# Moving three small second-layer matmul groups behind the last first-layer product of a step

## The chip, the cores and the metric

The kernel runs on one core of a Trainium2 chip. TensorE (PE) multiplies, with its weight loads (PEld) as a stream of their own; VectorE (DVE) and ScalarE (ACT) do everything elementwise; SyncE (SP) issues the DMAs. The metric is the device time of one execution in microseconds, as the median of several runs; less is better.

## The reference

```
qn = q / (norm(q, axis=1) + 1e-6);  kn = k / (norm(k, axis=1) + 1e-6)   # q, k, v: (4, 6080, 256)
s = kn^T @ qn / tau;  a = softmax(s)                                     # 256 x 256 for each batch
x = (v @ a).reshape(24320, 256)
h = x @ w_in                                                             # 256 -> 2048
g = 0.5 * h * (1 + erf(h / sqrt(2)))
out = g @ w_out                                                          # 2048 -> 256
```

For each of four batches a channel attention gives a 256 x 256 matrix; the attended values then pass a feed-forward layer with an exact GELU. All of it is in float32.

## The kernel before

The attention matrix is multiplied into `w_in` once for each batch, so that per token only two products are left: a first layer, `v` by the folded weights (256 to 2048), and a second layer, the GELU's output by `w_out` (2048 to 256). Every float32 operand is split into a high and a low part of a narrower format, and each product is three matmuls: high by high, high by low, low by high.

The tokens of a batch are cut into six pairs of column blocks, of 512 columns each (480 in the last pair). A pair is worked in eight **steps**, each for 256 of the 2048 hidden units. In all but 17 of the 192 steps the first layer uses a Strassen-Winograd scheme: seven products instead of eight 2 x 2 block products. The seven products are numbered 0 to 6 here; `first_products` issues them, three matmuls each, into two PSUM banks in turn (tile `h` in the profile). Products 0, 2, 4 and 6 accumulate in the bank `one`, products 1, 3 and 5 in the bank `two`. Between them the banks are read:

- ACT copies product 0 (`p1`), product 1 (`p5`), and the sum of products 0 and 2 (`u2`);
- after product 3, DVE adds `u2` to bank `two` (`added`, shown as `h<-h,u`); after product 4 it adds `p5` to bank `one` (`h<-h,p`); after product 5 it adds `p1` to bank `two` (`h<-h,p` once more). Each sum goes to a tile in SBUF, and ACT takes the GELU of it;
- after product 6, ACT takes the GELU straight from bank `one`.

Product 5 begins bank `two` anew, so it can start only when DVE has read the sum after product 3. Product 6 goes on accumulating in bank `one`, so it can start only when DVE has read the sum after product 4.

The second layer of a step is issued one step later, between the products of the next step, by the generator `second_products`: each `next(second)` issues one group of three matmuls. After a Strassen step it has eleven groups, numbered 0 to 10: four of full width (groups 0 to 3, tile `c`), then seven of half width, of which 4 and 5 go to the bank `p0`, 6 and 7 to `p1`, 8 and 9 to `c00` and 10 to `c01`. `count` holds 11 or 8.

From the second pair of the first batch on, each engine runs its instructions in the order in which the program issues them (`keep_in_program_order`). Whatever else there is to do, such as the attention of the next batch, the splits of the next `v` and the output merges, is put by tables into slots of the steps: `run(i, slot)` issues the jobs of a slot. Slots 0 to 5 come behind products 0 to 5, slot 7 (`EARLY`) behind product 6 and ahead of the remaining groups, and slots 6, 8 and 9 behind those. Two jobs of the softmax that TensorE does stand in slot 7: a broadcast matmul (`h<-diag,ones`) and four transposes (`h<-ident,t`), each once in batches 1 to 3 for the batch that follows. They write the bank that `bank()` hands out next, which is the one that products 1, 3 and 5 of the step used.

The order of TensorE's work in a step whose predecessor has eleven groups is thus, before the change: product 0, group 0, product 1, group 1, product 2, group 2, product 3, group 3, product 4, groups 4 and 5, product 5, groups 6 and 7, product 6, slot 7, groups 8 to 10.

Of the kernel before, what the change touches and what calls it, by code (L numbers as in the profile page):

```python
# [98 lines left out]
def channel_attention_gelu_ffn(ctx, tc, qk, kqt, vt, tau, w_in, w_out, out):  # L99
# [262 lines left out]
    def sum_wo(u):  # L362

        wo = wos[0, 1, u]
        x = pg.tile([P, 2, NT], F32, name="x", bufs=1)
        full = x[:, 0].rearrange("p (f c) -> p f c", f=2)
        s1, s2, s3, s4 = (x[:, 1, i * P:(i + 1) * P] for i in range(4))
        a11, a12, a21, a22 = (full[:, 1 - k, c * P:(c + 1) * P] for c in range(2) for k in range(2))
        tt = dve.tensor_tensor
        tt(out=full, in0=f32(wo[:, 0]), in1=f32(wo[:, 1]), op=ALU.add)  # L370
        yield
        tt(out=s1, in0=a21, in1=a22, op=ALU.add)
        tt(out=s3, in0=a11, in1=a21, op=ALU.subtract)
        tt(out=s2, in0=s1, in1=a11, op=ALU.subtract)
        tt(out=s4, in0=a12, in1=s2, op=ALU.subtract)
        yield
        new_ws((0, 1, u))
        ws = wss.pop((0, 1, u))
        hi, lo = (ws[:, i].rearrange("p s c -> p (s c)") for i in range(2))
        act.copy(out=hi, in_=x[:, 1])  # L380
        yield
        tt(out=lo, in0=x[:, 1], in1=f32(hi), op=ALU.subtract)
        nc.sync.dma_start(out=keep_sum[u], in_=f32(ws))
# [118 lines left out]
    def w_sums(g):  # L502

        tmp = wtmp.pop(g)
        a21, a11, a22, a12, s1, s2, s3, s4 = (tmp[:, i] for i in range(8))
        tt = dve.tensor_tensor
        tt(out=s1, in0=a21, in1=a22, op=ALU.add)
        tt(out=s3, in0=a11, in1=a21, op=ALU.subtract)
        tt(out=s2, in0=s1, in1=a11, op=ALU.subtract)
        tt(out=s4, in0=a12, in1=s2, op=ALU.subtract)  # L510
        w_both(whs[g][:, S1:], wls[g][:, S1:], tmp[:, 4:])
# [3 lines left out]
    def w_part(b, g, m):  # L515

        eh, el = state["e"]
        win = wins[b, g]
        if m == 0:
            wtmp[g] = pqk.tile([P, 8, 2, P], F32, name="hl", bufs=3)  # L520
        tmp = wtmp[g]
        cs = slice(m * P, (m + 1) * P)
        pwt = bank()
        for d in range(NCT):
            mm(pwt, eh[:, d, cs], win[:, 0, d], start=(d == 0), stop=False)
            mm(pwt, eh[:, d, cs], win[:, 1, d], start=False, stop=False)
            mm(pwt, el[:, d, cs], win[:, 0, d], start=False, stop=(d == NCT - 1))
        act.activation(out=tmp[:, 2 * m:2 * m + 2], in_=pwt.rearrange("p (q r c) -> p r q c", q=2, r=2),
                             func=AF.Copy, scale=state["rden"][:, m:m + 1])
        if m == NCT - 1:  # L530
            wins.pop((b, g))
        if b == 0:
            w_first(g, m, tmp)
            if (g, m) == (NWG - 1, NCT - 1):
                give(*state.pop("eh"))
# [78 lines left out]
    def strassen(b, p, u):  # L614
        return (b, p) > (0, 1) and (b, p, u) != (B - 1, NP - 1, NU - 1)
# [29 lines left out]
    def sums(n):  # L645

        h = n // 2
        x = state["x"]
        b11, b22, b21 = (x[:, k * h:(k + 1) * h] for k in (1, 2, 3))
        t3, t2, t4 = (x[:, k * h:(k + 1) * h] for k in (5, 6, 7))  # L650
        tt = dve.tensor_tensor
        hb = pg.tile([P, 3 * C], F32R, name="gh1", bufs=1)
        lb = pg.tile([P, 3 * C], F32R, name="gl1", bufs=1)
        ht = pg.tile([P, 4 * C], F32R, name="gh0", bufs=1)
        lt = pg.tile([P, 4 * C], F32R, name="gl0", bufs=1)
        state["blocks"]["b"], state["blocks"]["t"] = (hb, lb), (ht, lt)
        tt(out=x[:, 4 * h:6 * h].rearrange("p (k c) -> p k c", k=2),
           in0=x[:, h:3 * h].rearrange("p (k c) -> p k c", k=2),
           in1=x[:, 0:h].unsqueeze(1).broadcast_to([P, 2, h]), op=ALU.subtract)
        act.copy(out=hb[:, :3 * h], in_=x[:, h:4 * h])  # L660
        tt(out=t2, in0=t3, in1=b11, op=ALU.add)
        yield
        tt(out=t4, in0=b21, in1=t2, op=ALU.subtract)
        yield
        act.copy(out=ht[:, :4 * h], in_=x[:, 4 * h:8 * h])
        tt(out=lb[:, :3 * h], in0=x[:, h:4 * h], in1=f32(hb[:, :3 * h]), op=ALU.subtract)
        yield
        tt(out=lt[:, :4 * h], in0=x[:, 4 * h:8 * h], in1=f32(ht[:, :4 * h]), op=ALU.subtract)
# [196 lines left out]
    def load_unit():  # L865
        kind, g, d = units.pop(0)
        src = w_in64[:, d, g * NT:(g + 1) * NT] if kind == "in" else w_out64[:, g * 2 * C:(g + 1) * 2 * C]
        loaded.append((kind, g, d, load_w(src)))
# [11 lines left out]
    def narrow_unit():  # L880
        kind, g, d, raw = loaded.popleft()
        if kind == "in":
            if d == 0:
                new_win(0, g)
            win = wins[0, g]
            narrow(win[:, 0, d], win[:, 1, d], raw)
            if d == NCT - 1:
                keep(keep_in[g], win)
        else:
            new_wo((0, 0, g))  # L890
            wo = wos[0, 0, g]
            narrow(wo[:, 0].rearrange("p f c -> p (f c)"), wo[:, 1].rearrange("p f c -> p (f c)"), raw)
            keep(keep_out[g], wo)
# [73 lines left out]
    def ahead(b, p, u):  # L967

        def after(k):
            i = (b * NP + p) * NU + u + k  # L970
            return i // NU // NP, i // NU % NP, i % NU

        nxt = after(2)
        if nxt[0] < B and nxt[:2] != (0, 0):
            load_wo(nxt)
        nxt = after(1)
        if nxt[0] < B and strassen(*nxt):
            load_ws(nxt)
# [15 lines left out]
    def run(step, slot):  # L994
        for job in jobs.pop((step, slot), ()):
            job()

    def spread(gen, step, *slots):
        for x in slots:
            at(step + x // 10, x % 10, lambda: next(gen, None))  # L1000
# [73 lines left out]
    second, count, rest = iter(()), 0, iter(())  # L1074
    for i, (b, p, u) in enumerate(steps):
        plain = (b, p) == (0, 0)
        if (b, p) == (0, 1) and u == 0:
            for name in ("p0", "p1"):
                ring.remove(name)
            state["pinned"] = True  # L1080
        if (b, p) == (0, 1):
            spread(sum_wo(u), i, 0, 1, 2, 10)
        mine = strassen(b, p, u)
        for slot, _ in enumerate((plain_products if plain else first_products)(b, p, u)):
            for _ in range(1 if slot < 4 or count < 11 else 2):
                next(second, None)
            if slot < 2:
                next(rest, None)
            run(i, slot)
        run(i, EARLY)  # L1090
        for _ in second:
            pass
        run(i, 6)
        if mine:
            rest = sums(PAIRS[p][1])
            next(rest)
        if plain:
            for _ in range(paces[u] if u < len(paces) else 0):
                narrow_unit()
                if units:  # L1100
                    load_unit()
        ahead(b, p, u)
        if plain:
            if u % 2 == 0 and u // 2 + 1 < NWG:
                for m in range(NCT):
                    w_part(0, u // 2 + 1, m)
            if u % 2 == 0:
                w_sums(u // 2)
        run(i, EDGE)
        run(i, EDGE + 1)  # L1110
        if mine:
            next(rest)
        count = 11 if mine else 8
        second = second_products(b, p, u, state.pop("blocks"))
# [32 lines left out]
```

## Time and profile before

| what | value |
|---|---|
| median of 3 runs | 2141.93 us (2141.68 to 2142.57) |
| the profiled execution | 2142.28 us |
| its span, first to last instruction | 2140.4 us |
| PE / PEld busy | 2131.2 / 1828.8 us |
| DVE / ACT busy | 1768.9 / 1634.7 us |
| granted TensorE clock | 1.00 |

A busy PE includes matmuls that overlap, so a short pause of TensorE may not show as idle time; the distance from the start of one matmul to the start of the next says more. In the rows of the timeline the first number is the start in us from the start of the span, the second the length; `x2` joins two neighbours of one form; `[0.59 <-DVE h]` is idle time of the engine ahead of the instruction and what ended it. All the instructions that go through the kernel's recording helper carry its line, L171, so the tiles (`out<-in`) tell them apart.

### The profile page before, as it was taken

Reading aid. Unit: us, or ns where it says so; the run is one execution under the profiler, and the core shown is the slowest. Engines: PE = TensorE matmul, PEld = TensorE weight load, DVE = VectorE, ACT = ScalarE, POOL = GpSimd, SP = SyncE. Lnnn points to the kernel's source line nnn. Section 1 sums busy time; section 2 is a strip of 40 time slices with the busy share of each in tenths; the row PEclk is TensorE's granted clock in tenths of the full one; section 3 lists DMA queues with packets and bytes.
Section 4 is the critical chain, followed back from the end, with each engine's and each line's share of the span. In section 5 each row is a group of like instructions: output and inputs, shape, how many; then the busy total and the mean of one; then the engine's idle time right before and its main releaser. Section 6 shows DMA issues by size and latency. Waiting matters only on the chain.

```text
span 2140.4 us, 30621 instructions
## 1 busy us (share of the span) xinstructions
PE 2131.2 (100%) x11259; PEld 1828.8 (85%) x11259; DVE 1768.9 (83%) x2798; ACT 1634.7 (76%) x2695; POOL 1.3 (0%) x8
## 2 busy tenths in 40 slices
PE   9999999999999999999999999999999999999999
PEld 8777888888888888888888888888888888888888
DVE  6997878888788888888888878888788887787786
ACT  6667878878788788776778877877777777777775
POOL 0000000000000000000000000000000000000000
PEclk9999999999999999999999999999999999999999
DMA  9545656554255565644444655654344343343332
GB/s 381 189 158 177 226 177 207 191 202 154 106 200 199 173 212 187 206 159 156 147 151 165 214 172 204 207 175 140 137 140 165 111 155 120 117 155 119 119 138 88
DMA packets 111013, 363.75 MB, mean 170 GB/s; under 512 B 11792, under 2 KB 16016, under 8 KB 108816
## 3 DMA queue, kind: packets, MB, share of 16 engines
q1 hardware_dynamic: 110864, 361.81, 48.4%
q8 instruction: 88, 1.44, 0.3%
q14 instruction: 61, 0.50, 0.1%
HBM read 324.27 MB, written 37.49 MB: 169 GB/s over the span
## 4 chain that ended last, share of the span: by engine, by line
PE 92%; DVE 0%; DMA 0%; issue 0%; ACT 0%; DVEq 0%; ACTq 0%
PE h L171 47%; PE c L171 33%; PE p L171 12%; DMA wo<-keep_out 0%; DVE x L171 0%; DVE osb L171 0%; DVE hl L171 0%; DVE h L171 0%; ACT g L171 0%; ACT gh L171 0%; DVE v L171 0%; DVE gl L171 0%; DVEq L1143 0%; ACT osb L171 0%; ACTq L171 0%
## 5 line engine op out<-in xcount | busy, mean ns | idle before, releaser
L171 PE MATMUL c<-gh,wo 128*128 128x512 f32 (+3 forms) x2372 | 827.9, 359 | 0.6 <-DVE wo L171 0.6
L171 PE MATMUL h<-v,wh 128*128 128x512 f32 (+1 forms) x2624 | 814.4, 391 | 1.1 <-DVE h L171 1.1
L171 PEld LDWEIGHTS h<-v,wh 128*128 128x128 f32 x2624 | 455.4, 188 | 73.4 <-ACT p L171 2.2
L171 PE MATMUL h<-v,wl 128*128 128x512 f32 (+1 forms) x1312 | 513.4, 391 | 0.0
L171 PEld LDWEIGHTS c<-gh,wo 128*128 128x128 f32 x2372 | 445.8, 188 | 76.7 <-DVE wo L171 1.7
L171 DVE TENSOR_TENSOR gl<-x,gh 128x768 fp32r<-128x768 f32 (+1 forms) x350 | 376.6, 1076 | 57.4 <-ACT gh L171 57.4
L171 PE MATMUL c<-gl,wo 128*128 128x512 f32 (+3 forms) x1186 | 421.4, 355 | 0.8 <-DVE gl L171 0.8
L171 ACT ACTIVATE gh<-h 128x512 fp32r<-128x512 f32 (+1 forms) x402 | 251.5, 626 | 210.9 <-DVE h L171 192.6
L171 ACT CAST gh<-x 128x768 fp32r<-128x768 f32 (+1 forms) x350 | 327.9, 937 | 46.2 <-DVE x L171 26.9
L171 DVE TENSOR_TENSOR x<-x 128x256 f32<-128x256 f32 (+2 forms) x557 | 274.4, 495 | 80.5 <-ACT x L171 67.5
L171 DVE TENSOR_TENSOR gl<-g,gh 128x512 fp32r<-128x512 f32 (+1 forms) x418 | 284.3, 681 | 21.3 <-ACT g L171 18.1
L171 ACT COPY p<-h 128x512 f32<-128x512 f32 (+1 forms) x368 | 213.2, 579 | 108.4 <-PE h L171 106.8
L171 PEld LDWEIGHTS h<-v,wl 128*128 128x128 f32 x1312 | 246.4, 188 | 52.1
L171 DVE TENSOR_TENSOR h<-h,p 128x512 f32<-128x512 f32 (+1 forms) x368 | 250.8, 682 | 47.7 <-PE h L171 35.4
L171 PEld LDWEIGHTS c<-gl,wo 128*128 128x128 f32 x1186 | 222.7, 188 | 42.9 <-DVE gl L171 1.2
L171 ACT ACTIVATE g<-h 128x512 f32<-128x512 f32 (+1 forms) x402 | 245.8, 611 | 0.0
L171 PE MATMUL p<-gh,ws 128*128 128x256 f32 (+1 forms) x1050 | 240.3, 280 | 0.0
L171 ACT ACTIVATE x<-h 128x512 f32<-128x512 f32 (+1 forms) x350 | 204.3, 607 | 35.9 <-DVE h L171 32.4
L171 PEld LDWEIGHTS p<-gh,ws 128*128 128x128 f32 x1050 | 185.8, 189 | 8.0
L171 DVE TENSOR_TENSOR h<-h,u 128x512 f32<-128x512 f32 (+1 forms) x184 | 125.7, 683 | 74.9 <-PE h L171 73.4
L171 DVE TENSOR_TENSOR v<-v,v 128x512 fp32r<-128x512 f32 (+3 forms) x257 | 173.9, 677 | 0.5 <-ACT v L171 0.5
L171 PE MATMUL p<-gl,ws 128*128 128x256 f32 (+1 forms) x525 | 146.5, 279 | 0.0
(128 smaller groups left out, 1967.9 us busy)
## 6 DMA issues: line engine op xcount, KB each, us to landing
wo<-keep_out SPq DMA_DIRECT2D x184, 512.0 KB, 4.5
ws<-keep_sum SPq DMA_DIRECT2D x175, 512.0 KB, 3.6
raw<-qk SPq DMA_DIRECT2D x94, 512.0 KB, 4.3
raw<-kqt SPq DMA_DIRECT2D x72, 512.0 KB, 4.4
v<-vt SPq DMA_DIRECT2D x80, 256.0 KB, 3.3
out<-osb SPq DMA_DIRECT2D x40, 512.0 KB, 3.4
hl<-keep_in SPq DMA_DIRECT2D x12, 1024.0 KB, 5.6
raw<-w_in SPq DMA_DIRECT2D x8, 512.0 KB, 6.3
```

Of the source, the lines that this page charges most:

```text
L171: r = op(*args, **kw)
```

## The change

Behind each of products 0 to 5 one group is issued, whatever the count. With eleven groups the order becomes: product 4, group 4, product 5, group 5, product 6, slot 7, groups 6 to 10. Group 5 moves behind product 5, and groups 6 and 7 move behind product 6. With eight groups nothing changes.

```diff
         mine = strassen(b, p, u)
         for slot, _ in enumerate((plain_products if plain else first_products)(b, p, u)):
-            for _ in range(1 if slot < 4 or count < 11 else 2):
-                next(second, None)
+            next(second, None)
             if slot < 2:
                 next(rest, None)
             run(i, slot)
```

## The prediction

> **What bounds the kernel now.** I read the busy rows of the page first, then the chain and the waits, and then one step of the timeline, since the change only reorders TensorE's work inside a step.
>
> ```profile
> span 2140.4 us, 30621 instructions
> PE 2131.2 (100%) x11259; PEld 1828.8 (85%) x11259; DVE 1768.9 (83%) x2798; ACT 1634.7 (76%) x2695; POOL 1.3 (0%) x8
> PEclk9999999999999999999999999999999999999999
> L171 PEld LDWEIGHTS h<-v,wh 128*128 128x128 f32 x2624 | 455.4, 188 | 73.4 <-ACT p L171 2.2
> ws<-keep_sum SPq DMA_DIRECT2D x175, 512.0 KB, 3.6
> PEld h L171 <- DVE h L171: 3.1, 5, 1.4
> ```
>
> TensorE is busy 2131.2 of 2140.4 us, at the full granted clock in all 40 slices; nothing else can be the bound. The `ws` load happens once for each step whose second layer has eleven groups, so 175 steps are touched. The last row is the largest wait of the weight loads (PEld), which run ahead of the matmuls: 3.1 us in total, five times, against 175 steps. There is therefore almost nothing to win from a shorter wait, and the question is which new waits the new order makes.
>
> I number a step's first-layer products 0 to 6 and the second layer's groups 0 to 10 (0 to 3 wide, 4 to 10 small). Here is one step from product 4 on; PE is the matmuls, DVE the vector engine's sums:
>
> ```profile
> 352.76 0.62 PE L171 MATMUL h<-v,wh 128*128 128x512 f32 x2
> ...
> 353.45 0.28 PE L171 MATMUL p<-gh,wo 128*128 128x256 f32 x1
> 353.58 1.01 DVE L171 TENSOR_TENSOR osb<-c,osb 128x512 f32<-128x512 f32 x2
> ...
> 354.16 0.63 PE L171 MATMUL h<-v,wh 128*128 128x512 f32 x2
> 354.51 0.68 DVE L171 TENSOR_TENSOR h<-h,p 128x512 f32<-128x512 f32 x1
> ...
> 354.86 0.28 PE L171 MATMUL p<-gh,ws 128*128 128x256 f32 x1
> ...
> 355.45 0.30 PEld L171 LDWEIGHTS h<-v,wh 128*128 128x128 f32 x2
> 355.56 0.63 PE L171 MATMUL h<-v,wh 128*128 128x512 f32 x2
> ```
>
> Product 4 starts at 352.76, groups 4 and 5 at 353.45, product 5 at 354.16, groups 6 and 7 at 354.86, product 6 at 355.56; groups 8 to 10 follow it. So a pair of small groups takes 0.70 us (355.56 - 354.86), one 0.35, and a product 0.70. Products 4 and 6 use the same PSUM bank, and 6 accumulates onto what 4 left there, after DVE has read 4's result: that read is the sum `h<-h,p` at 354.51, done at 355.19. Product 6 starts 0.37 after it. That distance is the step's **slack**.
>
> **The change part by part.** It adds and removes no instruction: the same matmuls, weight loads, sums, activations and DMAs are issued, and the order on DVE, ACT and SP stays. On TensorE, group 5 moves behind product 5, and groups 6 and 7 behind product 6. Three times a step a small matmul still precedes a product, so matmul pitch changes by nothing. The cover is what changes: product 5 comes 0.35 us earlier relative to product 4, product 6 comes 0.70 earlier, and the tail behind product 6 grows by 0.70, so the next step's product 0 stays where it was.
>
> What is late then is DVE's sum of product 4, because it hangs on product 4 and on DVE's queue, and neither moves. In the step above DVE spends 1.01 us on two output merges (`osb<-c,osb`) ahead of it. How much slack product 6 needs beside the shift, two rows of an existing wait of this kind show:
>
> ```profile
> 162.29 0.68 DVE L171 TENSOR_TENSOR h<-h,u 128x512 f32<-128x512 f32 x1
> ...
> 163.02 0.30 PEld L171 LDWEIGHTS h<-v,wh 128*128 128x128 f32 x2 [0.59 <-DVE h L171]
> ```
>
> The sum ends at 162.97 and the weight load that waited starts at 163.02: 0.05 us. The weight load, which carries the wait, leads the matmul by 0.11 (355.45 to 355.56). So a step loses time when its slack is below 0.70 + 0.11 + 0.06 = **0.87 us**, and it loses the difference; where the groups come from a narrower pair (240 columns) they are 0.67 the two and the threshold is 0.83.
>
> I took the slack of product 6 in every step. An ordinary step, and then one of each kind that loses (sum of product 4, product 6):
>
> ```profile
> 2009.90 0.69 DVE L171 TENSOR_TENSOR h<-h,p 128x512 f32<-128x512 f32 x1 [0.62 <-PE h L171]
> 2011.81 0.63 PE L171 MATMUL h<-v,wh 128*128 128x512 f32 x2
> 1494.30 0.68 DVE L171 TENSOR_TENSOR h<-h,p 128x512 f32<-128x512 f32 x1
> 1495.36 0.63 PE L171 MATMUL h<-v,wh 128*128 128x512 f32 x2
> 1656.03 0.68 DVE L171 TENSOR_TENSOR h<-h,p 128x512 f32<-128x512 f32 x1
> 1657.19 0.62 PE L171 MATMUL h<-v,wh 128*128 128x512 f32 x2
> 1644.99 0.65 DVE L171 TENSOR_TENSOR h<-h,p 128x480 f32<-128x480 f32 x1
> 1646.05 0.60 PE L171 MATMUL h<-v,wh 128*128 128x480 f32 x2
> 1162.31 0.68 DVE L171 TENSOR_TENSOR h<-h,p 128x512 f32<-128x512 f32 x1
> 1163.44 0.63 PE L171 MATMUL h<-v,wh 128*128 128x512 f32 x2
> 1748.03 0.68 DVE L171 TENSOR_TENSOR h<-h,p 128x512 f32<-128x512 f32 x1
> 1749.37 0.63 PE L171 MATMUL h<-v,wh 128*128 128x512 f32 x2
> 1393.36 0.68 DVE L171 TENSOR_TENSOR h<-h,p 128x512 f32<-128x512 f32 x1
> 1394.82 0.63 PE L171 MATMUL h<-v,wh 128*128 128x512 f32 x2
> ```
>
> The first pair has 1.22 against 0.87: DVE stood idle and took the sum the moment product 4 was done, and nothing is lost. Then, with the number of steps of that kind (the kinds recur in each batch with the same slack to about 0.02):
> - merges ahead of the sum: 0.38, six steps from the one at 352.76 to this one: 6 x 0.49 = 2.9 us;
> - a copy of the output bank ahead of it, narrow groups: 0.48, three steps: 3 x 0.35 = 1.1;
> - weight sums and a `v` split ahead of it, narrow: 0.41, six steps: 6 x 0.42 = 2.5;
> - weight sums behind a split, wide: 0.45, two steps: 2 x 0.42 = 0.8;
> - one merge step with an emptier queue: 0.66, once: 0.2;
> - a copy or a `v` split: 0.78 to 0.81, seven steps: 7 x 0.07 = 0.5.
>
> Together 8.0 us in 25 steps. The other 144 steps without a softmax job lie between 0.88 and the 1.22 of the ordinary one, which is also the commonest, and lose nothing. Product 5's own wait (its bank is read by the sum of product 3) comes to at most 0.2 in the second kind, and lies inside what product 6 loses there.
>
> The remaining six steps are those of the softmax, where TensorE has a job between product 6 and the tail: a broadcast matmul (`h<-diag,ones`, three times) and four transposes (`h<-ident,t`, three times). Both write the bank of product 5, which DVE must have read:
>
> ```profile
> 489.22 0.69 DVE L171 TENSOR_TENSOR h<-h,p 128x512 f32<-128x512 f32 x1
> 489.96 0.70 PE L171 MATMUL h<-diag,ones 128*128 128x256 f32 x2
> 1035.19 0.68 DVE L171 TENSOR_TENSOR h<-h,p 128x512 f32<-128x512 f32 x1
> 1036.24 0.60 PE L171 MATMUL h<-ident,t 128*128 128x128 f32 x4
> ```
>
> The broadcast waits for that sum already: it ends at 489.91 and the matmul starts at 489.96. The sum itself stands behind other DVE work and doesn't move, so the whole 0.70 that product 6 comes forward is lost: 3 x 0.70 = 2.1 us. The transposes start 0.37 after their sum; they need 0.17 and would come 0.70 earlier, so 0.50 is lost where the sum stands still as here, and some 0.13 in the other two, whose sum waits for product 5 and comes 0.2 to 0.3 earlier with it: 0.8.
>
> **Sum:** 8.0 + 2.1 + 0.8 = 10.9 us. The profiled execution took 2142.28 us with a span of 2140.4, so it would become 2153.2; the median of the three runs lies 0.35 below it, which gives **2152.8 us**, 0.5% slower.
>
> No row shows this wait at product 6, so the price of one wait has two ends. If only the matmul, not its weight load, had to follow the sum, the 0.11 goes: the thresholds become 0.76 and 0.72, the kinds give 2.3, 0.7, 1.9, 0.6, 0.1 and nothing, with 2.1 and 0.4 from the softmax steps 8.1 in all, 2150.0. If the load has to be complete (mean 0.188), 0.08 more is lost in each of 28 places, 2155.4. I take 0.11, since the start of the load against the start of the matmul is what the rows show beside each other. A gain below nothing is excluded here, as a product can't start before its load.
>
> The Trainium skill, TensorE: Matmul & The Clock Gate, section "LDWEIGHTS (loading the stationary operand)", gives a load as its columns over 1.2 GHz, an estimate of 0.107 us for 128. By that the sum stays at 10.9; by the duration of the row it would be some 2.5 more.
>
> **The rivals.**
> 1. *The late sums come forward too* (not slower). It decides if DVE, in the 25 steps, is late through a queue that starts at the last step's products 5 and 6 and so starts 0.35 to 0.70 earlier. Then the 8.0 goes and 2.9 stay: 2144.8. For it: DVE is 83% busy. Against it: in the step at 352.76 what delays DVE hangs on merges, splits and earlier groups, whose places relative to product 0 stay. 7 in 100.
> 2. *The longer tail covers waits at the head of the next step* and nothing else happens. The price is at most all 3.1 us of the quoted wait: 2138.8, faster by less than 0.2%. Against it: the new order has its own waits. 2 in 100; 1 more for a gain beyond that.
> 3. *The clock drops.* If TensorE's short waits cost it the clock, each of the 31 places would run a product and a pair of groups at, say, half rate, 0.70 + 0.70 us more: 43 us on top of the 10.9, 2196. Against it: the clock row is full although a wait of 0.59 stood at 163.02. 2 in 100. The Trainium skill, TensorE: Matmul & The Clock Gate, section "A second HAM failure mode: psum-queue depth-cycling", tells of a kernel whose clock swung because TensorE idled briefly between groups while cycling PSUM banks; by that rule this rival would hold, and the trace, with its full clock, speaks against it.
> 4. *Each new wait makes another*, since ACT's activations stand behind DVE's sums: twice 10.9 gives 2163.7. Against it: a TensorE that is held gives DVE and ACT the same time to catch up. 5 in 100.
> 5. *The order on TensorE doesn't follow the source*: 2141.9. Against it: the step above has exactly the source's order. 1 in 100.
>
> **How the numbers follow.** The forecast keeps 82 in 100. Its range is the two ends, 2150.0 to 2155.4, widened by about the 0.9 us that the three runs before spread over: 2149.0 to 2156.5. That holds the 82, so it needn't reach to the rivals. A measurement of this kernel tells about 0.2% (4.3 us) from no change. Slower by more: forecast, rivals 3 and 4, 89 in 100. Within: rivals 1, 2 and 5, 10. Faster: 1.
>
> **What would show it.** In the profile after: the waits of PEld `h` for DVE `h` go from 3.1 us to some 14, in some 30 more places; the waits stand at product 6 in the steps with merges, copies, splits or weight sums, 0.35 to 0.5 us each, and not in the steps with slack 1.22; the tail behind `h<-diag,ones` has five groups and the next product starts 0.70 later relative to it. Without waits there, or with product 6 held in ordinary steps, the reasoning is wrong; with the clock below full, rival 3 holds.

## The result and the profile after

The changed kernel takes 2153.39 us (median of 4 runs, 2153.2 to 2154.28) against 2142.12 (4 runs, 2141.68 to 2142.57): 1.0054 times as long, with a 95% interval of 1.0042 to 1.0065. It is slower by 11.3 us; the forecast was 10.9 more, 2152.8. The profiled execution took 2153.26 us.

The page of the changed kernel, its busy rows, its clock and the chain that ended last:

```profile
span 2151.5 us, 30625 instructions
PE 2138.1 (99%) x11259; PEld 1830.2 (85%) x11259; DVE 1766.5 (82%) x2798; ACT 1622.7 (75%) x2695; POOL 1.3 (0%) x8
PEclk9999999999999999999999999999999999999999
...
PE 86%; DVE 5%; ACT 1%; issue 1%; DMA 0%; DVEq 0%; ACTq 0%
```

The chain of the kernel before:

```profile
PE 92%; DVE 0%; DMA 0%; issue 0%; ACT 0%; DVEq 0%; ACTq 0%
```

The number of matmuls is the same, the clock is full in every slice, and the span is 11.1 us longer. PE's busy time grew by 6.9 us of these, though no work was added, because part of each wait lies under the records of matmuls (the last section shows how). The chain says it better: DVE went from 0 to 5% of it, since TensorE is held there and the chain turns aside to the sum that held it. The waits, with total, number and longest, first of the weight loads and then of the matmuls:

```profile
PEld h L171 <- DVE h L171: 11.4, 24, 1.4
...
PE h L171 <- DVE h L171: 4.9, 18, 0.9
```

The first row was 3.1 us in five waits, the second 1.1 us in two. The step that the prediction quotes from product 4 on (there from 352.76) now reads:

```profile
353.77 1.01 DVE L171 TENSOR_TENSOR osb<-c,osb 128x512 f32<-128x512 f32 x2
...
354.01 0.64 PE L171 MATMUL h<-v,wh 128*128 128x512 f32 x2
...
354.70 0.68 DVE L171 TENSOR_TENSOR h<-h,p 128x512 f32<-128x512 f32 x1
354.72 0.28 PE L171 MATMUL p<-gh,ws 128*128 128x256 f32 x1
...
354.95 0.28 PE L171 MATMUL p<-gh,ws 128*128 128x256 f32 x1
...
355.44 0.30 PEld L171 LDWEIGHTS h<-v,wh 128*128 128x128 f32 x2 [0.41 <-DVE h L171]
355.44 0.73 PE L171 MATMUL h<-v,wh 128*128 128x512 f32 x2 [0.21 <-DVE h L171]
```

Product 5 starts at 354.01, the one group behind it at 354.72, and product 6 could start 0.35 later, at 355.07. The sum of product 4 ends at 355.38, held up by the same two merges as before, and 0.06 later the weight load of product 6 starts. An ordinary step (sums of products 4 and 5 on DVE, products 5 and 6 on PE) shows the opposite:

```profile
2020.93 0.69 DVE L171 TENSOR_TENSOR h<-h,p 128x512 f32<-128x512 f32 x1 [0.62 <-PE h L171]
...
2021.09 0.63 PE L171 MATMUL h<-v,wh 128*128 128x512 f32 x2
...
2022.14 0.68 DVE L171 TENSOR_TENSOR h<-h,p 128x512 f32<-128x512 f32 x1
2022.14 0.63 PE L171 MATMUL h<-v,wh 128*128 128x512 f32 x2
```

DVE waits for product 4, its sum ends at 2021.62, and product 6 starts at 2022.14, exactly 1.05 after product 5 (0.70 for the product, 0.35 for a group): slack 0.52 instead of 1.22, and nothing lost.

The broadcast of the softmax:

```profile
490.32 0.68 DVE L171 TENSOR_TENSOR h<-h,p 128x512 f32<-128x512 f32 x1
...
491.06 0.70 PE L171 MATMUL h<-diag,ones 128*128 128x256 f32 x2 [0.38 <-DVE h L171]
...
491.41 0.48 PE L171 MATMUL p<-gh,ws 128*128 128x256 f32 x1
```

It still starts 0.06 us after the sum of product 5, and five groups come behind it now (the first on `p`, group 6), where three did.

Lining up the start of product 0 of every step in the two traces gives where the 11.1 us arise, since the distance between the traces grows only in a step that loses:

```
kind of step (as in the prediction)        steps   forecast   measured
merges ahead of the sum                      6       2.9        2.9
copy of the output bank, narrow groups       3       1.1        1.1
weight sums and a split, narrow              6       2.5        2.6
weight sums behind a split, wide             2       0.8        0.8
merges, emptier queue                        1       0.2        0.2
copy or split, near the threshold            7       0.5        0.4
softmax, broadcast                           3       2.1        1.9
softmax, transposes                          3       0.8        0.7
all other places                                     0          0.4
```

The named places make 10.7 us of the 11.1. Of the 0.4 elsewhere 0.16 lie ahead of the first step that the change touches, so they are chance: the named places alone came out 0.2 under the forecast, and part of its nearness to 11.3 is luck.

### The profile page after: what moved, and what is told of

Same layout as the page of the kernel before. It is cut to its first block, busy times and chain, and to the rows that moved or that the text cites. A ratio compares the mean times of both kernels' runs of the same rounds, so it can differ in the third digit from the quotient of the medians.

```text
span 2151.5 us, 30625 instructions
## 1 busy us (share of the span) xinstructions
PE 2138.1 (99%) x11259; PEld 1830.2 (85%) x11259; DVE 1766.5 (82%) x2798; ACT 1622.7 (75%) x2695; POOL 1.3 (0%) x8
## 4 chain that ended last, share of the span: by engine, by line
PE 86%; DVE 5%; ACT 1%; issue 1%; DMA 0%; DVEq 0%; ACTq 0%
PE h L171 44%; PE c L171 31%; PE p L171 11%; DVE h L171 1%; DVE gl L171 1%; DVE osb L171 1%; DVE hl L171 1%; DVE x L171 1%; ACT gh L171 0%; DMA wo<-keep_out 0%; DVE v L171 0%; DVE small L171 0%; ACT x L171 0%; ACT hl L171 0%; ACT p L171 0%
## 5 line engine op out<-in xcount | busy, mean ns | idle before, releaser
L171 ACT ACTIVATE x<-h 128x512 f32<-128x512 f32 (+1 forms) x350 | 193.4, 600 | 19.0 <-DVE h L171 7.3
```

The source lines that it names most:

```text
L171: r = op(*args, **kw)
```

## The experiments

The theory: a step loses time only where DVE's sum (of product 4 for product 6, of product 5 for a softmax job) ends too late for the shifted product, by exactly the missing slack. Its first rival is a small cost of the new order in every step. Each run is timed against the kernel before on the same chip, whose median was 2142.23 us in the first four and 2142.25 in the last four.

**The new order only where it should cost.** LATE holds the 31 step numbers that the slacks before named.

```diff
-            next(second, None)
+            for _ in range(2 if slot > 3 and count > 8 and i not in LATE else 1):
+                next(second, None)
```

> The new order only in the 31 steps that the slack arithmetic named (25 with a late sum of product 4, six with a softmax job behind product 6), the old order in the other 144. Theory (the loss is the wait of product 6, or of the softmax job, for a sum on DVE that doesn't move): the whole loss stays, about 11 us over the kernel before, 2153. Rival (the new order costs a little in every step, by pitch or by weight loads): 31 of 175 parts of it, 2 us, 2144.

2153.03 us, 1.0053 times the kernel before (1.0039 to 1.0067): the whole loss, 10.8 us, from 31 of 175 steps.

**And only where it shouldn't**, `i in LATE` in the same line.

> The reverse: the new order in the 144 other steps, the old one in the 31. Theory: no loss, 2142 within 0.5 us, although product 6 comes 0.70 us earlier in 144 steps. Rival of a cost in every step: 144 of 175 parts, 9 us, 2151.

2142.56 us, 1.0 (0.9992 to 1.0009). The weight loads' largest wait, of this kernel:

```profile
PEld h L173 <- DVE h L173: 2.8, 5, 1.4
```

It is nearly that of the kernel before, 3.1 us in as many waits. The two runs together exclude a cost in every step: moving three groups is free in 144 steps, to within the 1.9 us of the interval's upper end.

**All seven small groups behind product 6.**

```diff
-            next(second, None)
+            for _ in range(0 if slot > 3 and count > 8 else 1):
+                next(second, None)
```

> All seven small groups behind product 6, so product 5 comes 0.70 us and product 6 1.40 us earlier than in the kernel before. Theory: the threshold goes from 0.87 to 1.57 us of slack, above the ordinary 1.22, so that every step loses 0.35 us or more; summed over the slacks of the profile before 83 us, and some 6 more in the six softmax steps: 89 us, 2231. Rival (a cost for each group moved): seven groups moved against three in the change, 11 x 7/3 = 26 us, 2168.

2231.03 us (2230.75 to 2231.11), 1.0414 (1.04 to 1.0429): 88.8 us where 89 were worked out from the slacks and 26 would follow from a cost for each group. Its waits, its clock, and one of its ordinary steps (sum of product 4, product 6):

```profile
PEld h L171 <- DVE h L171: 127.4, 219, 1.4
```

```profile
PEclk9999999999999999999999999999999999999999
```

```profile
1999.32 0.69 DVE L171 TENSOR_TENSOR h<-h,p 128x512 f32<-128x512 f32 x1 [0.62 <-PE h L171]
...
2000.06 0.74 PE L171 MATMUL h<-v,wh 128*128 128x512 f32 x2
```

Now product 6 waits in each of the 175 steps; in the one shown it starts 0.05 after a sum that DVE took as soon as it could. The 219 waits don't cost TensorE its clock, and they don't multiply: the loss is the sum of the missing slacks. Rivals 3 and 4 of the prediction fall with this run.

**The DVE work that makes the sum late, moved.** The output merges go behind the sum of product 4.

```diff
-    "end": (8, 10, 13, 13),
+    "end": (8, 10, 14, 14),
```

> The changed kernel with the two output merges of a pair one slot later, behind the sum of product 4 instead of ahead of it. Theory: the six steps with merges lose nothing (2.9 us) and the single one with an emptier queue neither (0.2): 2150.2. Rival (product 6 waits for something else than this DVE sum, such as ACT or a bank's first write): 2153.4 as with the change.

2151.23 us, 1.0042 (1.0029 to 1.0055): of the 3.1 us expected back, 2.2 came (2153.39 - 2151.23), and each of its five runs is below all four of the changed kernel. The step of before's 352.76, two output merges and their neighbours:

```profile
353.53 0.69 DVE L171 TENSOR_TENSOR h<-h,p 128x512 f32<-128x512 f32 x1
...
354.75 0.63 PE L171 MATMUL h<-v,wh 128*128 128x512 f32 x2
...
355.37 1.02 DVE L171 TENSOR_TENSOR osb<-c,osb 128x512 f32<-128x512 f32 x2
...
359.29 0.68 DVE L171 TENSOR_TENSOR sacc<-h,sacc 128x512 f32<-128x512 f32 x1
...
360.03 0.74 PE L171 MATMUL h<-v,wh 128*128 128x512 f32 x2
```

The sum ends at 354.22 and product 6 at 354.75 has no wait left, so in these steps the cause is confirmed. But DVE is later afterwards, and product 1 of the next step waits for the `sacc` sum that ends at 359.97 and frees its bank. Of the 0.49 in each of the six steps 0.32 come back, and the single step with the emptier queue loses nothing any more. In two other steps (weight sums behind a split, wide) product 5 now waits 0.24 us, beside the wait of product 6 that the changed kernel has there too, and each loses 0.26 more; what makes DVE later there is open. Lined up as above, these changes make 1.6 us; some 0.3 more of the 2.2 arose ahead of the first step that the change touches, by chance.

**Half the shift**, in two ways: one group behind product 4 and two behind product 5, or two and one.

```diff
-            next(second, None)
+            for _ in range(2 if slot > 4 and count > 8 else 1):
+                next(second, None)
```

> One small group behind product 4, two behind product 5, four behind product 6: products 5 and 6 both come 0.35 us earlier than in the kernel before. Theory: threshold of product 6 0.52 us, of product 5's own wait 0.52; by the slacks 2.3 us, and in the softmax steps 3 x 0.35 for the broadcast and some 0.2 for the transposes: 3.5 us, 2145.6. Rival (loss proportional to the shift of product 6): half of 11, 2147.7.

2145.77 us, 1.0016 (1.0007 to 1.0025), 3.5 us over the kernel before: the slacks' number and not half of 11.3. The other way, with `slot == 4`:

> Two small groups behind product 4, one behind product 5, four behind product 6: product 6 comes 0.35 us earlier, product 5 stays. Theory: as the run with one and two, less product 5's own wait: by the slacks 1.6 us, and 1.3 in the softmax steps: 2.9 us, 2145.0. If product 5's move matters by itself, the two runs differ by more than 0.7 us.

2145.42 us, 1.0014 (1.0005 to 1.0023), 3.2 us over. The two differ by 0.35 us, less than their intervals tell apart, so product 5's own wait for the sum of product 3 couldn't be measured by time. The traces do show it: lined up, the three steps with a copy of the output bank lose 0.23 to 0.24 us each with one and two, and 0.02 with two and one.

**More cover for product 6 than before**: three groups behind product 5, two left for the tail.

```diff
-            next(second, None)
+            for _ in range(slot - 2 if slot > 3 and count > 8 else 1):
+                next(second, None)
```

> Two small groups behind product 4, three behind product 5, two behind product 6: product 6 comes 0.35 us later than in the kernel before. Theory: no step of the kernel before waits at product 6, so nothing is won there, and the broadcast's wait of some 0.1 us in three steps goes: 2141.8, not to be told from the kernel before. Rival (more cover still helps): a gain of the size of the run with one and two, 3.5 us, 2138.6.

2145.1 us, 1.0013 (1.0005 to 1.0022): 2.9 us slower, where the theory had no change and the rival a gain. Both missed a wait at the other end of the tail. The waits of the weight loads, and one of the places (ACT's copy of product 1 of a step, and product 3, which goes on in the bank that the copy has read):

```profile
PEld h L171 <- ACT p L171: 6.3, 26, 0.3
PEld h L171 <- DVE h L171: 2.8, 5, 1.4
```

```profile
1747.26 0.57 ACT L171 COPY p<-h 128x512 f32<-128x512 f32 x1
...
1747.88 0.73 PE L171 MATMUL h<-v,wh 128*128 128x512 f32 x2
```

In the waits the second row is nearly as before; the first was 2.2 us in ten waits. The copy ends at 1747.83 and the product starts 0.05 later. What makes the copy late starts a step earlier, at ACT's GELU of product 6, here beside the product 0 that follows, first in this run and then in the kernel before (where the row joins it with the GELU ahead of it):

```profile
1743.21 0.60 ACT L171 ACTIVATE x<-h 128x512 f32<-128x512 f32 x1 [0.34 <-PE h L171]
...
1743.71 0.63 PE L171 MATMUL h<-v,wh 128*128 128x512 f32 x2
```

```profile
1739.56 1.22 ACT L171 ACTIVATE x<-h 128x512 f32<-128x512 f32 x2 [0.32 <-DVE h L171]
...
1741.04 0.63 PE L171 MATMUL h<-v,wh 128*128 128x512 f32 x2
```

The GELU ended 0.26 us ahead of product 0 and now ends 0.10 behind its start, so it is 0.36 later. What ACT does after it is later too, up to the copies of the next step's first products, and there TensorE waits. The tail behind product 6 is cover for ACT as the groups behind 4 and 5 are cover for DVE.

**The softmax's jobs behind the tail**, on the changed kernel.

```diff
-    "soft": (3, 10, 11, 16, 17, 18, 21, 22, 26, 37),
+    "soft": (3, 10, 11, 16, 18, 18, 21, 22, 26, 36),
```

> The changed kernel with the softmax's broadcast and transposes behind the tail instead of ahead of it, so that five groups cover the sum of product 5. Theory: the 2.9 us of these six steps go, unless the next step's product 1, which needs the same bank, then waits for DVE's reads of it (up to 0.3 us in each): between 2150.5 and 2152. Rival (these six steps lose nothing of their own): 2153.4.

2154.07 us, 1.0054 (1.004 to 1.0068): nothing came back, so by time alone the rival's number came out. The waits that changed:

```profile
PEld h L171 <- DVE h L171: 7.4, 18, 1.4
PEld h L171 <- ACT p L171: 4.8, 10, 0.9
...
PEld h L171 <- DVE sacc L171: 1.5, 3, 0.5
```

The wait for the sum of product 5 is gone (11.4 to 7.4 us in the first row), but the jobs' own readers on ACT and DVE are later, and the first products of the following steps wait for these engines: the second row rose from 2.1 and the third is new, together 4.2 us for the 4.0 that went. I had allowed 0.3 us a step for this; it was all of the 0.45 or so. This run says that the place of these jobs isn't the remedy; it doesn't speak against the loss ahead of it, which the trace shows.

No run is faster than the kernel before.

## Why the prediction was right, point by point

- **The bound.** Right: TensorE had nothing to win, and the run with the new order in 144 steps shows it: 2142.56.
- **No cost of the order itself.** Right, by the same run.
- **The sum of product 4 doesn't move, and the threshold is 0.87 us of slack.** Right: in the 25 steps the end of that sum, counted from the start of product 4, is where it was to within 0.03 us, and each kind of these steps loses what was worked out to some 0.1 us, as the table shows. It holds at two other thresholds too, 0.52 (3.5 us by time against 3.5 expected, and 3.2 against 2.9) and 1.57 (88.8 against 89). So the choice of 0.11 us for the weight load's lead was right: by the lower end the change would have cost 8.1. The upper end is 13.5 as it was forecast, but its own terms (0.08 more in each of 28 places) give 13.1, 2155.0 instead of 2155.4; both lie above the 11.3 measured.
- **Where the steps come from.** The count of 175 is right. The seven products, though, run in 184 steps, as many as the trace has sums `h<-h,u`; the 17 steps named ahead of the prediction are those whose second layer isn't split into eleven groups, and only the first eight have a first layer without the seven products.
- **The softmax steps.** The mechanism was right; the broadcast cost 0.64 us a step on average (0.61 to 0.68) in place of 0.70, the transposes 0.7 in all in place of 0.8. The sum of product 5 that the broadcast waits for did move a little: it ended 9.07 us behind product 0 of its step and now ends 9.00 behind it. In the run with the new order in 31 steps alone it stays at 9.07, and there the broadcast costs 0.67 to 0.72. So the new order in the steps ahead brought DVE 0.07 forward, the mechanism of rival 1 in small.
- **What would show it.** The wait of PEld for DVE `h` was to reach some 14 us in 30 more places; it shows 11.4 in 19 more. The losses are there, but this row is idle time of the weight loads: a load lasts 0.19 and one follows another 0.12 later, so the first 0.07 of each delay is hidden behind the end of the load before, and the seven losses of 0.07 leave no row. In the three steps with a copy of the output bank the wait is split, some 0.15 at product 5 and 0.05 at product 6, and of these only one, of 0.16, is in the row. The three broadcasts waited in the kernel before too (0.37 then, 0.82 now), so they are no new places.
- **The rivals.** The late sums didn't come forward (2144.8 would have been the time); the longer tail covered nothing that cost; the clock stayed full even with 219 waits; the waits didn't multiply. The Trainium skill, TensorE: Matmul & The Clock Gate, section "A second HAM failure mode: psum-queue depth-cycling", tells of a clock that swings under frequent short idle times between groups. This case's trace shows no such swing: with weight-load waits of 0.37 to 1.23 us at product 6 of each of 175 steps, the granted clock is full in all 40 slices. The section "LDWEIGHTS (loading the stationary operand)" of the same page of the Trainium skill gives, as an estimate, 0.107 us for a weight load of 128 columns. As a duration the trace doesn't agree with it, since the record of a load lasts 0.19; the figure lies near the 0.11 by which a load leads its matmul.

## What to carry to other kernels

Where one engine is busy all the time, work between a producer and the reuse of its buffer is cover, and its worth is read from one number for each place: the distance from the end of the buffer's reader to the next writer. In this kernel an order could be changed freely as long as the shift, with the 0.17 us that the hand-over and the weight load's lead need, stayed below the smallest distance, and the price beyond it was the sum of what was missing, in the few steps where the reader's engine was late with other work. Shifting cover from one place takes it from another, so the distances at both ends of the moved work have to be read.

## What the runs showed that I had not expected

A matmul whose weight load waited is recorded as starting with its load (both at 355.44 in the changed kernel), and the second of the pair comes 0.34 later where 0.23 is usual, so about 0.11 us of such a wait counts as busy time of TensorE. Some 0.16 more is hidden ahead of it: the last matmul of the group is recorded from 354.95 to 355.23, past the 355.07 at which product 6 could have started. Of the 0.48 lost there only 0.21 is idle time of the matmuls. That is why PE's busy time rose by 6.9 us with no work added, and why idle time alone would have shown less than half of the loss: the matmuls' row of waits grew from 1.1 to 4.9 us, the span by 11.1.
